# Loading the decay factors first on ScalarE's queue, and making four operand sums one in a slot, in a fused attention and mixture kernel

## The chip, the core and the metric

The kernel runs on one core of one Trainium2 chip. The metric is the device time of one execution in microseconds. Eight runs of the kernel before the change gave a median of 1192.49 us, from 1191.36 to 1193.86.

## The reference

Two computations follow one another, all in 32-bit floats. The first is attention with a decay for each head (4 batches, 8 heads, 768 positions, 64 features), in blocks along the sequence with a running state:

```
intra = (q_b k_b^T * lam^(i-j) for i >= j) v_b
inter = (q_b * lam^(i+1)) kv_state
out_b = intra + inter
kv_state = lam^block * kv_state + (k_b * lam^(block-1-j))^T v_b
```

Its output, rearranged to x of 3072 rows and 512 columns, goes through four experts whose outputs are mixed with normalised probabilities:

```
p = domain_probs / (sum(domain_probs) + 1e-9)
out = sum over e of p[:, e] * (relu(x @ w1[e]) @ w2[e])       # w1: 512x1024, w2: 1024x512
```

## The kernel before

**Units and stages.** Rows come in three groups g of 1024, and a unit (g, e) is one group with one expert. First comes the attention of group 0 (the loop at L1226), then the hidden layer of unit (0,0), written directly (`direct_product`, loop at L1287), then a loop over the twelve units (L1327). While a unit's second product (`second_product`, with w2) runs, the first product (`first_product`, with w1) of the following unit is put between it, and a few steps of the next group's attention as well.

**Seven products for eight.** Every 2x2 block product is made with seven products of sums of blocks, and the first product does that twice, one scheme inside the other. The outer products are M1 to M7; each needs an outer block of x (B11, B21, B22 or a sum T1 to T4, `B_OF`, L86) and from it again four inner sums T3, T1, T2, T4 of quarter blocks of 128x256 (`T_OPS`, L186). For later units these inner sums are made on GpSimd and kept in DRAM. For unit (0,1), the second one, `own_x` (L1095) makes them on VectorE, in place, and returns the views; the products read them straight from SBUF, and a list named `late` stores them to DRAM eight slots afterwards for the units behind (L1125).

**Slots.** A product index i (seven of them in a unit) has eight slots x. In slots 0, 2, 4 and 6 PE makes a part of the second product (eight matmuls), which VectorE adds into `acc` (L909 or L912). In slots 1, 3 and 5 PE makes two inner products of the first product, in slot 7 one. They alternate between two PSUM banks, g1 and g3, and go on accumulating in the same bank: an inner product may begin only when the one two before it has been read out of that bank by VectorE (`m<-pg,m`, L852 by way of L95) or ScalarE (L850). Bank g1 takes the first, third, fifth and seventh.

**What orders VectorE.** Engines work in the order in which the program writes. After the matmuls of a slot and their read-outs, `rest()` takes one step off the list `background` (sums of hidden blocks, attention's masks and scalings), and at the slot's end `pump()` (L143) runs chores that have come due. A chore named `mine[m]` (L1271, L1311 to L1318) makes unit (0,1)'s operands for product m: four sums of w1 on GpSimd and, by `own_x`, four sums of x on VectorE, all written at that one place. `take` (L485) pops the first entry of a list and runs it.

**The beginning.** The loads of q and k for the first two chunks of 128 rows are shared between SyncE's and ScalarE's DMA queues (`load`, L111: the half r = 1 goes through ScalarE for n < 2). After chunk 0's loads ScalarE's queue brings the eight decay factors `lam`, copied to all partitions (L402). VectorE makes from them the mask table `s_decay` (eight scans, L426) and the powers `q_decay` (seven doubling steps, L439). Chunk n goes through `turn` (transposes of q and k, L530), `scores` (L552, then masks `st<-sp,s_decay`) and `values` (L575 to L588); `turn` also writes a scaling `qs<-qT,q_decay` on VectorE and one of k on GpSimd (L505). In the loop `turn` runs one chunk ahead of `scores`, and `scores` one ahead of `values`.

Of the kernel before, what the change touches and what calls it, by code (L numbers as in the profile page):

```python
# [22 lines left out]
def kernel(  # L23
# [30 lines left out]
    nc = tc.nc  # L54
# [88 lines left out]
    def pump(pace=1.0, force=False):  # L143
        while results:
            results.pop(0)()
        while late and (force or late[0][0] <= now[0]):
            late.pop(0)[1]()
        begins = chores and (force or free[0] <= now[0])
        while queue and (force or queue[0][0] <= now[0] or begins and len(queue) > LEFT):
            queue.pop(0)[1]()  # L150
        if begins:
            begin = free[0] = max(free[0], now[0] - 1)
            was = max(busy[0], now[0])
            chores.pop(0)()
            free[0] = max(free[0], begin + max(pace * (busy[0] - was), 1))
# [240 lines left out]
            load(n, "kv")  # L396

    lam_bc = consts.tile([P, H], FP32, name="lam_bc")
    for n, names in ((0, "qk"), (1, "qk"), (0, "v"), (2, "qk"), (1, "v"), (3, "qk")):
        load(n, names)  # L400
        if (n, names) == (0, "qk"):
            nc.scalar.dma_start(out=lam_bc[:], in_=lam.partition_broadcast(P))  # L402
    raw_w1(0, "A11")
    load(2, "v")
    load(3, "v")
# [416 lines left out]
    def first_product(g, e, m, blocks, tags):  # L822

        while (g, e, m) not in fed:
            pump(force=True)
        xs, ws = fed.pop((g, e, m))
        settle(m, blocks)
        old = {
            "M1": None, "M5": None, "M6": blocks.get("M1"), "M2": blocks.get("M1"), "M7": blocks.get("U2"),
            "M3": blocks.get("U4"), "M4": blocks.get("U3"),  # L830
        }[m]
        new = {n: small("m" + n) for n in ("11", "12", "21", "22")} if m in ("M1", "M5", "M6") else old
        banks = {}

        def inner(i):
            t = tags[0] if i in ("M1", "M6", "M5", "M3") else tags[1]
            fresh = i in ("M1", "M7", "M2")
            if fresh:
                banks[t] = bank(t, "p" + t)
            p = banks[t]  # L840
            for j in range(2):
                nc.tensor.matmul(  # L842
                    out=p[:, j * 256:(j + 1) * 256], lhsT=ws[i][:, j * P:(j + 1) * P], rhs=xs[i],
                    start=(fresh and j == 0), stop=True, skip_group_check=True,
                )
            at, begins = READ[i]
            if not begins:
                tt(nc.vector, new[at][:], p[:], new[at][:], ALU.add)
            elif old is None:
                nc.scalar.copy(out=new[at][:], in_=p[:])  # L850
            else:
                tt(nc.vector, new[at][:], p[:], old[at][:], ALU.add)  # L852
            if m in OUT and (at == "12" or not begins):
                nc.scalar.activation(out=new[at][:], in_=new[at][:], func=AF.Relu)  # L854
                if g == LAST:
                    gated(e, *OUT[m], at, new[at])

        return [lambda i=i: inner(i) for i in INNER] + [lambda: finished(g, e, m, blocks, new)]
# [233 lines left out]

    x_tile = {}

    def own_x(m):  # L1095


        name = B_OF[m]
        blk = x_now[name]
        b = {f"B{i + 1}{j + 1}": blk[:, i, j * 256:(j + 1) * 256] for i in range(2) for j in range(2)}  # L1100
        if name in x_tile:
            t = x_tile[name]
            for n, (o, x, y) in {
                "T3": (t[:, 4], "B22", "B12"), "T1": (t[:, 1], "B12", "B11"), "T2": (t[:, 5], "B22", "T1"),
                "T4": (t[:, 6], "B21", "T2"),
            }.items():
                b[n] = o
                tt(nc.vector, o, b[x], b[y], ALU.subtract)
            pieces = ((0, 1), t[:, 0:1]), ((1, 4), t[:, 4:7]), ((4, 7), t[:, 1:4])
        else:  # L1110
            if m == "M1":
                s = [opool.tile([P, 2, 256], FP32, name="acc") for _ in range(2)]
                parts = ((1, 3), s[0][:]), ((3, 5), s[1][:])
                s = [x[:, i] for x in s for i in range(2)]
            else:
                s = stage.tile([P, 4, 256], FP32, name="ops", tag="st")
                parts = (((1, 5), s[:]),)
                s = [s[:, i] for i in range(4)]
            for n, x, y, op in T_OPS:
                b[n] = s[SLOT[n]]  # L1120
                tt(nc.vector, b[n], b[x], b[y], op)
            pieces = (
                ((0, 1), blk[:, 0:1, 0:256]), *parts, ((5, 7), blk[:, 1].rearrange("p (a f) -> p a f", a=2)),
            )
        late.append((now[0] + 8, keep_own(("x", 0, m), x_ops[0, MS.index(m)], pieces)))  # L1125
        return {i: b[B_OF[i]] for i in B_OF}

    def own_w1(m):
# [97 lines left out]
    for i in range(CPG + 2):  # L1226
        if i == 6:
            chores.extend((*prepare_w2(0), *(raw[n] for n in ("A11", "A22", "A21"))))
        more = list(between.get(i, ()))
        order = [(turn, 0), (scores, 1), (values, 2)]  # L1230
        if i == 3:
            order[0:2] = order[1::-1]
        for f, lag in order:
            n = i - lag
            if more and lag == 0 and i < CPG:
                more.pop(0)()
            if 0 <= n < CPG:
                f(n, pairs[n % 3])
            if i < 2 and lag == 0:
                warm(3 - i)  # L1240
            if i == 6 and lag == 2:
                sum_w1(0, "S1", "A21", "A22", ALU.add)
                sum_w1(0, "S3", "A11", "A21", ALU.subtract)
                own_blocks["M1"] = own_x("M1")
            if i == 7 and lag == 2:
                sum_w1(0, "S2", "S1", "A11", ALU.subtract)
                sum_w1(0, "S4", "A12", "S2", ALU.subtract)
            if i == 8 and lag == 0:
                x_sums(("T1", 0))
            if i == 9 and lag == 2:  # L1250
                x_sums(("T1", 1))
            if more and (lag == 2 or i >= CPG):
                more.pop(0)()
            now[0] += 1
            pump()
        while more:
            more.pop(0)()
        if i + 4 < CPG:
            load(i + 4)
        if i < 3:  # L1260
            for name in (("A12",), ("A21",), ("A22",))[i]:
                raw_w1(0, name)
        if i == 5:
            nc.scalar.dma_start(out=probs[:], in_=moe_domain_probs.rearrange("(t p) e -> p t e", p=P))
# [22 lines left out]
    for m in SEQ0[2:]:  # L1287
        if m == SEQ0[-1]:
            for _ in range(2):
                feed2(*fill2.pop(0))  # L1290
        work = direct_product(m, blocks, ("g1", "g3")) if m != "M5" else [m5[1], *m5[3:]]
        for x, f in enumerate(work):
            f()
            for y in sums_then.get((m, x), ()):
                y()
            rest()
            if x < len(work) - 1:
                now[0] += 1
                pump(0.75)
            if m in SEQ0[-2:]:  # L1300
                trickle()
# [25 lines left out]
    for at, (g, e) in enumerate(units):  # L1327
# [14 lines left out]
        for i in range(7):  # L1342
# [30 lines left out]
            for x, part in enumerate(order):  # L1373
                for f in part:
                    if f:
                        f()
                now[0] += 1
                if joins:
                    joined()
                elif (ahead or x % 2 == 0 and x + i) and not (at == len(units) - 2 and i == 6 and x == 7):  # L1380
                    rest()
                if nested or nests:
                    take(aside)
                if nested and ahead and x in (1, 3) and fill3:
                    feed3(*fill3.pop(0))
                if turned_back and x > 0:
                    y = turned_back.pop(0)
                    if y:
                        give(*y[:2], ("s0", "s1"), *y[2:])
                if x == 0 and at * 7 + i >= 6 and fill:  # L1390
                    feed(*fill.pop(0))
                if at == 0 and x == 0 and i < AHEAD:
                    load(CPG + i)
                if steps and (at > 0 or i > 1) and (x == 5 or (x == 2 and i in (1, 3, 5) and at not in (0, 3))):
                    steps.pop(0)()
                if x % 2:
                    trickle()
                pump(PACE[g])
# [32 lines left out]
```

## Time and profile before

| What | Value |
|---|---|
| Median of 8 runs | 1192.49 us (1191.36 to 1193.86) |
| The eight | 1191.36, 1191.47, 1191.71, 1191.95, 1193.04, 1193.13, 1193.23, 1193.86 |
| The profiled execution's own time | 1193.13 us |
| Its span, first to last instruction | 1191.2 us |
| Outside the span | 1.9 us |
| VectorE, GpSimd, ScalarE busy | 67%, 53%, 23% of the span |
| Mean granted TensorE clock | 0.998 of full speed |
| DMA | 324.23 MB, 272 GB/s over the span |

Times in a trace line are the start from the span's begin and the duration, both in microseconds, then engine, line, operation, tile written and tiles read. What stands in square brackets is how long the engine had been idle before and what released it. PE is TensorE, DVE is VectorE, ACT is ScalarE, POOL is GpSimd, SPq and ACTq are the queues that issue DMAs. A clock of 0.50 in a row of windows means that TensorE ran at half speed there.

### The profile page before, as it was taken

To read this page: it belongs to the slowest core of one execution; us is meant where nothing else is said; L and a number is where in the kernel's file an instruction comes from. 1 tells how busy PE (TensorE), PEld (TensorE's weight loads), DVE (VectorE), ACT (ScalarE), POOL (GpSimd) and SP (SyncE) were. 2 spreads that over 40 slices of the span, in tenths; PEclk is the share of its full clock that TensorE was granted. 3 is DMA by queue.
4 is the path that set the end of the run, shared out by engine and by line. 5 is a ranking of instruction groups with operands and counts; after the bars stand their busy time and mean duration, and the time that the engine had idled before them with its cause. 6 is when DMAs were issued, how large, how long until landed. Compare 5 with 4: busy or idle time off the path is not lost.

```text
span 1191.2 us, 17870 instructions
## 1 busy us (share of the span) xinstructions
PE 1179.2 (99%) x6559; PEld 1024.9 (86%) x6559; DVE 793.5 (67%) x1330; ACT 274.7 (23%) x502; POOL 630.8 (53%) x600
## 2 busy tenths in 40 slices
PE   8999999999999999999999999999999999999998
PEld 7888888888888888888888888888888888888887
DVE  6676786468467847647856774773665676777784
ACT  3332122112211201311120120121243342341232
POOL 2666238439457900045344565416584683783884
PEclk9999999999999999999999999999999999999999
DMA  9698799999999997899997989898986657566542
GB/s 226 179 277 241 229 297 319 352 318 351 350 356 325 330 296 226 249 293 298 310 324 244 293 294 308 281 326 281 317 281 248 258 189 271 208 243 239 212 169 79
DMA packets 261927, 324.23 MB, mean 272 GB/s; under 512 B 117296, under 2 KB 203216, under 8 KB 261840
## 3 DMA queue, kind: packets, MB, share of 16 engines
q1 hardware_dynamic: 252288, 320.40, 80.9%
q10 hardware_dynamic: 9552, 2.69, 1.0%
q8 instruction: 52, 0.85, 0.3%
q14 instruction: 35, 0.29, 0.1%
HBM read 237.69 MB, written 89.54 MB: 275 GB/s over the span
## 4 chain that ended last, share of the span: by engine, by line
PE 93%; DVE 3%; DMA 2%; issue 0%; POOL 0%; ACT 0%; ACTq 0%; SPq 0%; DVEq 0%
PE pg L842 38%; PE q L896 31%; PE pq L1068 13%; PE pM L1173 2%; PE sp L552 2%; PE op L580 2%; PE pc L1173 2%; DMA w_ops<-ops 1%; PE op L575 1%; PE op L588 1%; DMA ws_in<-w_ops 1%; DVE m L95 1%; PE pM L1038 1%; PE qp L530 0%; PE kp L530 0%
## 5 line engine op out<-in xcount | busy, mean ns | idle before, releaser
L842 PE MATMUL pg<-xs_in,ws_in 128*128 128x256 f32 x1960 | 469.7, 380 | 0.8 <-DVE m L95 0.8
L842 PEld LDWEIGHTS pg<-xs_in,ws_in 128*128 128x128 f32 x1960 | 371.2, 190 | 52.8 <-DVE m L95 1.8
L95 DVE TENSOR_TENSOR m<-pg,m 128x512 f32<-128x512 f32 x451 | 308.2, 688 | 107.8 <-PE pg L842 100.9
L896 PE MATMUL q<-w2t,hS 128*128 128x256 f32 x1024 | 243.4, 380 | 0.0
L896 PEld LDWEIGHTS q<-w2t,hS 128*128 128x128 f32 x1024 | 193.2, 190 | 27.0 <-issue 0.2
L912 DVE SCALAR_TENSOR_TENSOR acc<-q,gate,acc 128x256 f32<-128x256 f32 x192 | 92.5, 482 | 169.2 <-PE q L896 168.7
L896 PE MATMUL q<-w2t,m 128*128 128x256 f32 x768 | 182.7, 381 | 0.0
L896 PEld LDWEIGHTS q<-w2t,m 128*128 128x128 f32 x768 | 144.8, 190 | 20.5 <-issue 0.3
L854 ACT ACTIVATE m<-m 128x512 f32<-128x512 f32 x132 | 82.9, 630 | 286.2 <-DVE m L95 285.4
L95 POOL TENSOR_TENSOR m<-m,xT 128x512 f32<-128x512 f32 x64 | 80.7, 1277 | 72.7 <-ACT m L854 54.6
L95 POOL TENSOR_TENSOR kn<-kn,s_decay 128x512 f32<-128x512 f32 x20 | 21.9, 1099 | 142.4 <-DMA across<-in_k_dram 78.3
L95 DVE TENSOR_TENSOR sums<-pq,sums 128x256 f32<-128x256 f32 x154 | 64.8, 422 | 45.9 <-PE pq L1068 40.0
L850 ACT COPY m<-pg 128x512 f32<-128x512 f32 x88 | 51.6, 586 | 177.0 <-PE pg L842 174.4
L1068 PE MATMUL pq<-acc,w2t 128*128 128x256 f32 x352 | 86.6, 379 | 0.0
L95 POOL TENSOR_TENSOR ops<-w2b 128x256 f32<-128x256 f32 x24 | 18.1, 776 | 117.8 <-DMA w2b<-in_moe_w_dram 110.8
L1068 PEld LDWEIGHTS pq<-acc,w2t 128*128 128x128 f32 x352 | 66.8, 190 | 9.3 <-issue 0.3
L95 POOL TENSOR_TENSOR acc<-hT,hT 128x512 f32<-128x512 f32 x32 | 40.3, 1274 | 30.9 <-PE pq L1068 29.0
L95 POOL TENSOR_TENSOR w2o<-w2b 128x512 f32<-128x512 f32 x32 | 40.6, 1291 | 22.9 <-DMA w2b<-in_moe_w_dram 16.8
L787 ACT ACTIVATE m<-m 128x512 f32<-128x512 f32 x44 | 27.7, 631 | 101.5 <-DVE m L95 101.5
L95 DVE TENSOR_TENSOR hS<-m,m 128x512 f32<-128x512 f32 x56 | 45.2, 811 | 4.9 <-ACT m L854 4.9
L95 DVE TENSOR_TENSOR m<-m,m 128x512 f32<-128x512 f32 x56 | 47.2, 844 | 0.0
L593 ACT COPY xT<-op 128x256 f32<-128x256 f32 x48 | 17.1, 372 | 120.1 <-PE op L580 114.4
(152 smaller groups left out, 1393.1 us busy)
## 6 DMA issues: line engine op xcount, KB each, us to landing
xs_in<-x_ops SPq DMA_DIRECT2D x70, 896.0 KB, 6.5
ws_in<-w_ops SPq DMA_DIRECT2D x70, 896.0 KB, 8.7
w2t<-w_ops SPq DMA_DIRECT2D x66, 256.0 KB, 6.8
w2t<-w_sums SPq DMA_DIRECT2D x64, 256.0 KB, 3.9
w_ops<-ops SPq DMA_DIRECT2D x28, 512.0 KB, 5.5
w2t<-in_moe_w_dram SPq DMA_DIRECT2D x48, 256.0 KB, 3.7
w2b<-in_moe_w_dram SPq DMA_DIRECT2D x32, 256.0 KB, 5.8
w_sums<-w2o SPq DMA_DIRECT2D x16, 512.0 KB, 4.7
```

Of the source, the lines that this page charges most:

```text
L95: eng.tensor_tensor(out=o, in0=a, in1=b, op=op)
L552: nc.tensor.matmul(out=sp[r][:, ac * C:(ac + 1) * C], lhsT=hc(kT)[half[r], ac], rhs=hc(qT)[half[r], ac], start=True, stop=True,)
L580: nc.tensor.matmul(out=op[r][half[x], a * C:(a + 1) * C], lhsT=vn[:, 4 * r + 2 * a + x], rhs=hc(st[r])[:, 2 * a + x], start=(first and a = ...
L593: nc.scalar.copy(out=xT[:, 2 * r:2 * r + 2, c * C:(c + 1) * C], in_=op[r][:, 0:2 * C].rearrange("p (a t) -> p a t", t=C),)
L787: nc.scalar.activation(out=o[:], in_=o[:], func=AF.Relu)
L842: nc.tensor.matmul(out=p[:, j * 256:(j + 1) * 256], lhsT=ws[i][:, j * P:(j + 1) * P], rhs=xs[i], start=(fresh and j == 0), stop=True, skip ...
L850: nc.scalar.copy(out=new[at][:], in_=p[:])
L854: nc.scalar.activation(out=new[at][:], in_=new[at][:], func=AF.Relu)
L896: nc.tensor.matmul(out=p[:, s * DH:(s + 1) * DH], lhsT=h[A_OF[m]][:, c * 256 + s * P:c * 256 + (s + 1) * P], rhs=fed2[g, e, m][uu][:, c], ...
L912: nc.vector.scalar_tensor_tensor(out=o, in0=x, scalar=w, in1=o, op0=ALU.mult, op1=ALU.add)
L1068: nc.tensor.matmul(out=p[:, 0:256], lhsT=fed3[e, m, x // 2][:, x % 2, c * P:(c + 1) * P], rhs=b[B_OF[i]][:, c * 256:(c + 1) * 256], start= ...
L1173: nc.tensor.matmul(out=p[:, s * 256:(s + 1) * 256], lhsT=a[c][:, f:f + P], rhs=b[:, c, j * 256:(j + 1) * 256], start=(s == 0 and c == 0 an ...
```

## The change

Two edits. The load of `lam` is issued ahead of chunk 0's q and k on ScalarE's queue, where it was third. And `own_x` no longer writes its four sums at once, except for product M1: it puts them on a list `own_sums`, from which the direct stage (L1299) and the first unit (after `rest()`, ahead of the slot's `pump()`) take one in each slot. `first_product` takes all that are still missing of its own product before it uses them, and the store of the operands does so too.

```diff
     lam_bc = consts.tile([P, H], FP32, name="lam_bc")
+    nc.scalar.dma_start(out=lam_bc[:], in_=lam.partition_broadcast(P))
     for n, names in ((0, "qk"), (1, "qk"), (0, "v"), (2, "qk"), (1, "v"), (3, "qk")):
         load(n, names)
-        if (n, names) == (0, "qk"):
-            nc.scalar.dma_start(out=lam_bc[:], in_=lam.partition_broadcast(P))
...
         while (g, e, m) not in fed:
             pump(force=True)
+        while (g, e) == (0, 1) and to_do[m]:
+            take(own_sums, True)
         xs, ws = fed.pop((g, e, m))
...
-    def own_x(m):
+    to_do, own_sums = {}, []
+
+    def own_x(m, at_once=False):
...
+        steps = to_do[m] = []
+
+        def ready():
+            while steps:
+                take(own_sums, True)
+
+        def sub(o, x, y):
+            def f():
+                steps.pop()
+                tt(nc.vector, o, x, y, ALU.subtract)
+
+            steps.append(f)
...
-                tt(nc.vector, o, b[x], b[y], ALU.subtract)
+                sub(o, b[x], b[y])
...
-                tt(nc.vector, b[n], b[x], b[y], op)
+                sub(b[n], b[x], b[y])
...
-        late.append((now[0] + 8, keep_own(("x", 0, m), x_ops[0, MS.index(m)], pieces)))
+        work = list(steps)
+        if at_once:
+            for f in work:
+                f()
+        else:
+            own_sums.extend(work)
+        keep = keep_own(("x", 0, m), x_ops[0, MS.index(m)], pieces)
+        late.append((now[0] + 8, lambda: (ready(), keep())))
         return {i: b[B_OF[i]] for i in B_OF}
...
-                own_blocks["M1"] = own_x("M1")
+                own_blocks["M1"] = own_x("M1", True)
...
                 now[0] += 1
+                take(own_sums)
                 pump(0.75)
...
                     take(aside)
+                if at == 0:
+                    take(own_sums)
```

## The prediction

> **What bounds the kernel now.** I read the page's first row, then the waits of PE, then the chain of waits, the windows and the timeline at the two places where PE waits.
>
> ```profile
> PE 1179.2 (99%) x6559; PEld 1024.9 (86%) x6559; DVE 793.5 (67%) x1330; ACT 274.7 (23%) x502; POOL 630.8 (53%) x600
> ```
>
> ```profile
> PE pg L842 <- DVE m L95: 2.6, 3, 1.8
> PE op L580 <- DVE st L95: 2.4, 3, 2.1
> ```
>
> PE is busy for all but 12 of 1191.2 us, so an edit off PE can only win from those 12 and from a slow clock. Two waits stand out (total, times, longest): 2.1 us for the first mask st, and 1.8 us for one read-out. Everything that shortens them moves the rest forward: no later PE wait is for a DMA.
>
> The first wait, in the chain of waits (start, duration) and in the windows (busy PE, PEld, DVE, ACT, POOL, then the granted clock):
>
> ```profile
> 1.85 3.94 DMA lam_bc<-in_lam_dram
> 5.90 2.63 DVE s_decay L426 x8
> 8.80 0.96 DVE q_decay L439
> 9.78 0.99 DVE q_decay L439
> 11.50 1.05 DVE q_decay L439
> 13.10 0.69 DVE qs L95
> 13.79 1.21 DVE st L95 x2
> ```
>
> ```profile
> 13.00:14.00 1.00, 0.00 (x0) 0.00 (x0) 0.90 (x2) 0.00 (x0) 0.00 (x0) 1.00 0.71 235
> 16.00:17.00 1.00, 1.00 (x19) 0.89 (x16) 0.79 (x2) 0.21 (x1) 0.00 (x0) 0.50 0.39 93
> 17.00:18.00 1.00, 1.00 (x10) 0.99 (x10) 0.42 (x1) 0.37 (x1) 0.00 (x0) 0.50 0.24 56
> ```
>
> DVE works without a break from the landing of lam to the mask, so that landing sets the end. Three of the seven powers take 1 us instead of 0.2 to 0.3, each beside one of POOL's scalings of k. PE ends at 12.34, starts again at 14.45, and a microsecond later its clock is halved; in quarter-microsecond windows it is 0.50 from 15.48 to 18.87. Those 3.39 us cost 1.70 us of PE.
>
> The second wait, in the timeline:
>
> ```profile
> 124.92 0.75 DVE L95 TENSOR_TENSOR ops<-xT 128x256 f32<-128x256 f32 x2
> ...
> 134.71 3.54 DVE L95 TENSOR_TENSOR xt<-xt 128x256 f32<-128x256 f32 x4
> 138.18 0.47 DVE L909 TENSOR_SCALAR acc<-q,gate 128x256 f32<-128x256 f32 x1
> 138.57 0.81 DVE L95 TENSOR_TENSOR m<-m,m 128x512 f32<-128x512 f32 x1
> 139.31 1.28 DVE L95 TENSOR_TENSOR m<-pg,m 128x512 f32<-128x512 f32 x2
> 140.13 1.10 PE L842 MATMUL pg<-ops 128*128 128x256 f32 x4 [1.83 <-DVE m L95]
> ...
> 160.43 3.06 DVE L95 TENSOR_TENSOR xt<-xt 128x256 f32<-128x256 f32 x4
> 163.84 0.48 DVE L912 SCALAR_TENSOR_TENSOR acc<-q,gate,acc 128x256 f32<-128x256 f32 x1 [0.35 <-PE q L896]
> ```
>
> The four sums for M7 come right before a read-out that PE needs. They take 0.87 us each because POOL works then; without POOL a sum costs 0.33 to 0.46 (124.92). The sums for M4 (160.43) hurt nobody: they fill a pause in which PE does attention, and DVE is idle behind them for 0.35 us.
>
> **Part 1: lam first.** Nothing is added; one issue moves ahead of two. ScalarE's issues take 0.51 to 0.55 us, so lam goes out at 0.73 instead of 1.85. It lands at 4.67 if it needs its 3.94 us again, and at 3.2 to 3.7 if it needs the 2.5 to 3.0 us of the first q loads, with no packets ahead of it. I take 4.67, a gain of 1.12. What it moves back: the r = 1 halves of q and k of chunk 0, by 0.53 us. q's would land at about 4.3 against a transpose at 5.37; k's landed at 5.07 and would at 5.6, against 5.80. Chunk 1's issues stay fourth and fifth, and the stall of the fifth (until 3.77) stays. SP's queue isn't touched. So nothing is paid.
>
> DVE then scans from 4.78 to 7.41 and starts the powers at 7.68. POOL's first scaling (1.06 us) starts at 7.55 and blocks the first power until 8.64; its second needs the transposed k of chunk 1, at 8.8, and blocks another until 9.9. The third still comes at 11.33, and by then the other powers (0.18, 0.2, 0.3, 0.43) are done at about 11.1, so one of three collisions goes. qs starts at 11.2 and st at 11.8; PE can start at 12.5 to 12.6. PE's own order allows 12.34. The gain is 1.9 us (1.12 if all three collisions stay, 2.27 if PE never pauses).
>
> **The clock.** The Trainium skill (TensorE: Matmul & The Clock Gate, "Why this matters for your kernels") says that the clock falls after pauses of over about 3 us. By it, a pause of 2.1 us costs no clock, and the change wins nothing there. The row says otherwise: in the 3.4 us before 15.48 PE was idle for 2.3, and the clock fell. The same page's Part 1 says that the activity window runs freely and so differs from run to run; the eight times fit that, four at 1191.4 to 1192.0 and four at 1193.0 to 1193.9, 1.7 us apart, which is half of 3.39. The pause of 1.83 us at 138.3, by my count of such windows from 15.48 inside one, left the clock at 1.00. A pause of at most 1.2 us is below that, so I follow the row: the dip goes in every run. That is 1.70 us against the profiled run and 0.85 against the median.
>
> **What is late next.** PE would come 3.6 us earlier to the transposes of chunk 4, at 20.76 for k instead of 24.36. SP's queue is stuck in one issue for 4.25 us (12.77 to 17.02), so the second half of that k is issued at 18.16 and lands 2.9 us later, at 21.06. PE waits 0.3 us. The raw w1 block lands at 17.1, before its use (22.09 less 3.6). Part 1 and the clock: 1.9 + 1.7 - 0.3 = 3.3 us (2.8 to 3.4).
>
> **Part 2: the sums.** M1 is unchanged. M5's sums are made right before use and are taken together by the force in the first product: no change. M6's go into idle DVE time. The number of sums is the same; only their place changes, so it is a matter of who stands behind each. I went through DVE's and PE's order slot by slot from 118 to 178 us (read-out 0.60 apart, acc 0.40, background 0.60 or 0.80 beside POOL, sum 0.36 or 0.87; 0.20 from PE to DVE, 0.14 back). For the kernel before, this recurrence gives one stall of 2.26 us where the trace has 1.83 and 0.13 shortly after. With the sums spread:
> - M7's stall goes. Its sums fall behind acc and the background step, one to a slot, and the read-outs finish 0.1 to 0.3 us before PE asks.
> - M2's fourth sum now comes at 133.5, beside POOL (0.87), ahead of the read-out that was at 133.51. That ends at 135.04, and PE, due at 134.68, starts at 135.18: 0.50.
> - M4's sums leave the idle pause and go into slots 6 and 7 of their product and 0 and 1 of the next, where DVE is 91% busy (163.7 to 177.7). Two of them beside POOL put the read-out at 168.05, and PE waits 0.69.
> - M3's sums cost 0.07 at most.
>
> So 2.26 goes and 1.26 comes. I scale both by the 1.96 that the trace shows: the gain is 0.8 us. From the other sides: 1.96 if no sum stands in a read-out's way, and -0.2 if each stall doubles. The added force and the store cover the same sums; the store is due eight slots later and they are done in four, so SP's queue waits for nothing new.
>
> **The sum.** 1193.13 - 3.3 - 0.8 = 1189.0 us. Against the median that is 3.5 us or 0.29% (0.2%, or 2.4 us, is about what a measurement of this kernel can tell from no change).
>
> **The rivals.**
> - The spreading costs nothing: 1193.13 - 3.3 - 1.96 = 1187.9. For it: DVE has idle time in most slots. Against: the two dense stretches. 0.15.
> - Only a part comes. All three collisions stay, the pause of 1.0 us still halves the clock in some runs, or the sums' stall only moves: 1192.49 - 1.1 with nothing else is 1191.4, and with half the clock's gain 1190.5. For it: the rule of a free window; DVE is full from 132.3 to 146.8. 0.25, a fifth of it beyond 0.2%.
> - Slower: the sums, beside POOL everywhere and in dense slots, hold up read-outs. A read-out may come 0.7 us late before PE waits (1.73 of the slot between, less 0.2, 0.68 and 0.14), and a sum beside POOL is 0.87. If the sixteen of M2, M7, M3 and M4 cost 13.9 us and 8 of it reach PE, the time is 1187.9 + 8 = 1195.9. It decides from 4.6 us of new stalls on. Against it: POOL idles from 117.8 to 130.6 and from 138.8 to 159.9. 0.05.
> - The change doesn't do what it says: the force in the first product takes all sums in a bunch. Then part 2 gives nothing and the time is 1189.8. But M7 has eight slots for four sums; this lies within the likeliest case's range.
>
> The likeliest case, 1188.4 to 1189.9, has 0.55. Faster by over 0.2% (under 1190.1): 0.55 + 0.15 + 0.05 = 0.75; within 0.2%: 0.20; slower: 0.05. The range goes from 1187.8 to 1190.8 and leaves out some 0.05 below and 0.15 above.
>
> **What would show it.** Right: lam issued at 0.73, the scan starting at 3.3 to 4.8, PE's wait for st under 1.2 us, no clock of 0.50 in the first 40 us, a short wait of kp for k of chunk 4 near 21 us, no wait of 1.8 us near 138 less the shift, and waits of L842 for DVE of 0.3 to 0.7 in the products M2 and M3 of unit (0,1). Wrong: a clock dip that stays with a pause of 1 us; a scan that starts after 5.5 because another thing than the place in the queue delays lam; waits for DVE in unit (0,1)'s products that sum to over 2 us.

## The result and the profile after

The changed kernel takes 1188.76 us (median of 12 runs, 1187.79 to 1189.73). The kernel before, in 32 runs on the same chips, takes 1192.22 us (1190.41 to 1194.17). The ratio is 0.9970, with a 95% interval from 0.9962 to 0.9977: 3.5 us or 0.3% faster, clear of no change. The profiled execution of the changed kernel took 1189.16 us with a span of 1187.3 us. Line numbers after differ from those before by one, and behind `own_x` by more (L842 is L843 here, L530 is L529, L1173 is L1196).

The page's first row and PE's waits after (total, times, longest):

```profile
PE 1178.3 (99%) x6559; PEld 1023.6 (86%) x6559; DVE 791.9 (67%) x1330; ACT 274.7 (23%) x502; POOL 629.0 (53%) x600
```

```profile
PE pg L843 <- DVE m L95: 1.2, 3, 0.5
PE kp L529 <- DMA kn<-in_k_dram: 0.5, 2, 0.4
PE op L579 <- DVE st L95: 0.2, 1, 0.2
```

Both long waits are gone. The first mask is no longer waited for (the 0.2 us for an `st` is a wait between 30 and 100 us that the kernel before has too), and no single wait for a read-out is over 0.5. A wait for k of chunk 4 is new. The beginning, in the timeline after:

```profile
0.73 0.45 ACTq L399 DMA_DIRECT2D lam_bc<-in_lam_dram  x1
4.40 2.63 DVE L425 TENSOR_TENSOR_SCAN s_decay<-lam_bc,ident 128x128 f32<-128x128 f32 x8 [3.40 <-DMA lam_bc<-in_lam_dram]
7.30 3.41 DVE L438 TENSOR_TENSOR q_decay<-q_decay 128x4 f32<-128x4 f32 x7
10.81 0.69 DVE L95 TENSOR_TENSOR qs<-qT,q_decay 128x512 f32<-128x512 f32 x1
11.42 1.28 DVE L95 TENSOR_TENSOR st<-sp,s_decay 128x512 f32<-128x512 f32 x2
12.24 1.39 PE L579 MATMUL op<-st,vn 128*64 128x128 f32 x16
21.05 0.63 PE L529 MATMUL kp<-ident,kn 128*128 128x128 f32 x4 [0.39 <-DMA kn<-in_k_dram]
```

Lam goes out first, the scans start 1.5 us earlier, the seven powers take 3.41 us instead of 4.19 (one meeting with POOL less), and the first values follow the scores at 12.24 without a pause. The windows after (length, busy time of PE, PEld, DVE, ACT and POOL with their instructions, PE's clock, DMA share, GB/s) have no halved clock there:

```profile
13.00:14.00 1.00, 1.00 (x28) 0.96 (x24) 1.00 (x3) 0.37 (x1) 0.00 (x0) 1.00 1.13 318
16.00:17.00 1.00, 1.00 (x22) 0.69 (x22) 1.00 (x2) 0.89 (x2) 0.71 (x1) 1.00 1.09 251
17.00:18.00 1.00, 1.00 (x28) 1.00 (x26) 1.00 (x2) 0.34 (x1) 0.35 (x1) 1.00 0.65 149
```

And unit (0,1)'s sums, in the timeline after:

```profile
123.57 0.41 DVE L95 TENSOR_TENSOR ops<-xT 128x256 f32<-128x256 f32 x1
...
130.23 0.94 DVE L95 TENSOR_TENSOR ops<-xT,ops 128x256 f32<-128x256 f32 x1
131.09 0.68 DVE L95 TENSOR_TENSOR m<-pg,m 128x512 f32<-128x512 f32 x1
131.82 1.13 PE L843 MATMUL pg<-xT,w1b 128*128 128x256 f32 x4 [0.26 <-DVE m L95]
133.43 0.94 DVE L95 TENSOR_TENSOR xt<-xt 128x256 f32<-128x256 f32 x1
134.29 1.28 DVE L95 TENSOR_TENSOR m<-pg,m 128x512 f32<-128x512 f32 x2
136.23 0.41 DVE L95 TENSOR_TENSOR xt<-xt 128x256 f32<-128x256 f32 x1
...
155.61 3.06 DVE L95 TENSOR_TENSOR xt<-xt 128x256 f32<-128x256 f32 x4
```

M7's sums (xt from 133.43) stand singly between read-outs. M2's fourth (130.23) takes 0.94 beside POOL, where the first (123.57) takes 0.41, and holds up the read-out behind it; PE is idle for 0.26 ahead of the inner product that needs it. M4's four at 155.61 are still in one piece.

How far PE is ahead of the kernel before, by the start of the same instructions in the two timelines:

| Instruction | Before | After | Ahead by |
|---|---|---|---|
| kp of chunk 4 | 24.36 (from the chain) | 21.05 | 3.3 |
| first matmul of the second product, unit (0,0) | 93.23 | 89.95 | 3.28 |
| first matmul in unit (0,1)'s product M7 | 149.26 | 144.44 | 4.82 |
| last inner product before the nested group | 883.03 | 878.29 | 4.74 |
| first matmul of the nested group | 883.89 | 879.86 | 4.03 |
| last transpose | 1186.95 | 1182.99 | 3.96 |

So 3.3 us come from the beginning, 1.5 from the sums, and 0.7 is lost at one place near 879 us, where the timeline after says only "issue":

```profile
879.86 1.10 PE L1069 MATMUL pq<-m,w2t 128*128 128x256 f32 x4 [0.50 <-issue]
```

No other profiled run here has that wait, though three of them contain the whole change too. So nothing speaks for the change as its cause; what it was stays open.

### The profile page after: what moved, and what is told of

Read it like the earlier page. It is cut to its first block, busy times and chain, and to the rows that moved or that the text cites. A ratio compares the mean times of both kernels' runs of the same rounds, so it can differ in the third digit from the quotient of the medians.

```text
span 1187.3 us, 17869 instructions
## 1 busy us (share of the span) xinstructions
PE 1178.3 (99%) x6559; PEld 1023.6 (86%) x6559; DVE 791.9 (67%) x1330; ACT 274.7 (23%) x502; POOL 629.0 (53%) x600
## 4 chain that ended last, share of the span: by engine, by line
PE 92%; DVE 3%; SPq 2%; DMA 1%; issue 0%; ACT 0%; ACTq 0%; DVEq 0%
PE pg L843 38%; PE q L897 31%; PE pq L1069 13%; PE pc L1196 2%; PE op L579 2%; PE sp L551 1%; SPq L123 1%; PE pM L1196 1%; DVE hS L95 1%; DVE m L95 1%; PE op L574 1%; DMA w_ops<-w2b 1%; PE op L587 1%; PE pM L1039 1%; SPq L341 0%
## 5 line engine op out<-in xcount | busy, mean ns | idle before, releaser
L843 PE MATMUL pg<-xs_in,ws_in 128*128 128x256 f32 x1960 | 469.7, 380 | 1.0 <-DVE m L95 0.9
L843 PEld LDWEIGHTS pg<-xs_in,ws_in 128*128 128x128 f32 x1960 | 371.2, 190 | 53.0 <-DVE m L95 2.4
L95 DVE TENSOR_TENSOR m<-m,m 128x512 f32<-128x512 f32 x56 | 49.8, 889 | 0.0
L95 POOL TENSOR_TENSOR acc<-hT,acc 128x512 f32<-128x512 f32 x32 | 40.7, 1273 | 7.4 <-PE pq L1069 5.4
```

The costliest lines, as they stand in the source:

```text
L95: eng.tensor_tensor(out=o, in0=a, in1=b, op=op)
L843: nc.tensor.matmul(out=p[:, j * 256:(j + 1) * 256], lhsT=ws[i][:, j * P:(j + 1) * P], rhs=xs[i], start=(fresh and j == 0), stop=True, skip ...
```

## The experiments

The theory: the two edits are separate and add up; the first wins the pause and the clock, the second M7's burst. The rivals: the dip of the clock has another cause; the sums only move the stall. The kernel before was timed beside each set: 1192.23 us for the first four, 1192.38 for the next three, 1193.15 for the last two.

**Lam first, alone.** The diff's first hunk, and nothing else.

> The kernel before with the first edit alone: lam ahead of chunk 0 on ScalarE's queue, the sums still four at once. Theory (the two edits are separate and add up): PE's wait of 2.1 us for the first mask is down to 0.2 at most, no clock of 0.50 after the warm-up, a new wait of kp for the k of chunk 4 of about 0.4 us near 21 us, and the wait of 1.8 us for M7's burst stays. The profile's PE is 3.3 us ahead at chunk 4; the median is some 2.4 us under the kernel before (2.0 to 3.3). Rival (the clock's dip has nothing to do with this pause): the dip stays in about half of the runs and the median is 1.6 us under.

Measured: 1190.24 us, ratio 0.9980 (0.9971 to 0.9989), 2.0 us faster. The pause is gone and M7's wait of 1.8 us is there. At chunk 4 PE waits twice in this profile, and is 2.35 us ahead of before instead of 3.3 (its timeline, PE's rows):

```profile
20.75 0.63 PE L529 MATMUL qp<-ident,qn 128*128 128x128 f32 x4 [0.46 <-DMA qn<-in_q_dram]
22.01 0.63 PE L529 MATMUL kp<-ident,kn 128*128 128x128 f32 x4 [0.63 <-DMA kn<-in_k_dram]
```

The gain is at the lower end of what was expected. In this profile chunk 4's landing took 1.1 us of it back, against 0.4 in the profile of the changed kernel; whether it does so in the other runs is not shown. The interval is 1.3 to 3.5 us, so the median does not tell the theory's 2.4 from the rival's 1.6. What speaks against the rival is the clock, which the third experiment takes up.

**The sums spread, alone.** The changed kernel with the load of lam back in its old place.

> The kernel before with the second edit alone: sums one in a slot, lam where it was. Theory: M7's wait of 1.83 us gives way to one of 0.26 in front of M2's first inner product, so 1.5 us are won at unit (0,1), and the pause of 2.1 us near 13 us stays, with the halved clock in part of the runs. Median 1.5 us under the kernel before. By the recorded prediction's sum for this part it would be 0.8 us, with a wait of 0.7 us in the product M3. Rival (the sums' gain needs the earlier start): below 0.5 us.

Measured: 1190.94 us, ratio 0.9986 (0.9978 to 0.9995), 1.3 us faster. Between 120 and 145 us PE has one wait for a read-out, of 0.3 us. The gains of the two halves, 2.0 and 1.3, add up to 3.3, against 3.5 for both. In this profile lam happened to land earlier than before, and the pause was shorter; the clock still fell, as this kernel's timeline and then its windows show:

```profile
13.75 0.44 PE L580 MATMUL op<-st,vn 128*64 128x128 f32 x4 [1.48 <-DVE st L95]
```

```profile
11.00:14.40 3.40, 1.76 (x24) 1.22 (x22) 3.26 (x6) 0.86 (x2) 1.29 (x1) 1.00 0.99 261
...
14.60:17.70 3.10, 3.10 (x38) 2.98 (x36) 1.92 (x4) 0.74 (x2) 0.00 (x0) 0.50 0.56 127
```

In the 3.40 us from 11.00 PE was busy for 1.76; from 14.60 on its clock is 0.50, until about 17.8.

**The pause filled, the wait left.** PE does dummy matmuls where it was idle:

```diff
+            if i == 2 and lag == 2:
+                warm(7)
             if 0 <= n < CPG:
                 f(n, pairs[n % 3])
```

> The kernel before with seven dummy matmuls of zeros (of 128 columns, as the warm-up's) written on PE ahead of the first values, so that PE is busy in its pause near 13 us while the wait for the mask itself stays; what the kernel computes is the same. Theory (the pause is what halves the clock): no clock of 0.50 from 15.5 to 18.9 in the profile, and none of the upper runs: the median is about 0.85 us under the kernel before, a run with the dip being 1.7 us longer. Rival (the clock falls for another reason, such as the first real load on PE): the dip stays, and the median is that of the kernel before within 0.3 us.

Measured: 1191.53 us (1190.84 to 1192.66), ratio 0.9996 (0.9987 to 1.0004). The median is 0.7 us lower, but the interval holds no change; the scatter is what tells. The fillers are there, the values start at 14.35, nearly as before (14.45), and the clock stays, as this kernel's timeline shows and then its windows of PE alone (length, PE busy, its clock, DMA share, GB/s):

```profile
12.50 1.83 PE L414 MATMUL zp<-xT 128*128 128x128 f32 x14
14.35 0.44 PE L580 MATMUL op<-st,vn 128*64 128x128 f32 x4
```

```profile
11.00:14.40 3.40, 3.38 (x37) 1.00 0.98 242
...
16.00:17.00 1.00, 1.00 (x24) 1.00 0.65 148
```

The runs of the kernel before beside it can be sorted by their mean granted clock. Six of 27 have 0.998 and average 1193.34 us; ten have 1.000 and average 1191.40; a half-speed stretch of 3.4 us in 1191 would lower the mean by 0.0014. (A second such stretch at the kernel's very end, up to 2.3 us of it in these traces, takes up to 0.001 more in any kernel, so 0.998 needs the dip and 0.999 can be either.) With the pause filled no run of eleven has 0.998, the average is 1191.6, and none is over 1192.7 us, where nine of the 27 are over 1193. With lam first none of eleven has 0.998; with the sums alone, where the pause stays, five of eleven. Eleven runs alone could be chance. Taken together, 21 of the 62 runs of the kernel before that the three sets have show 0.998, and none of the 60 runs of the seven kernels in which PE does not pause there. The pause halves the clock, in part of the runs.

**Only M7's sums spread.** All others at once, as before:

```diff
-        if at_once:
+        if at_once or m != "M7":
```

> The changed kernel with only M7's sums one in a slot; those of M5, M6, M2, M3 and M4 are written at once, as before. Theory (only M7's burst cost PE time, and the wait of 0.26 us comes from M2's fourth sum, moved in front of a read-out): no wait of PE for a read-out between 100 and 180 us is left, and the median is 0.2 to 0.3 us under the changed kernel. Rival (spreading the others too is what keeps the read-outs on time): a wait of 0.3 us or more comes at M3's burst, in the second half of the product M2, and the median is the changed kernel's or above.

Measured: 1188.51 us (1187.97 to 1189.55), ratio 0.9965 (0.9952 to 0.9977). In the profile PE has no wait at all between 100 and 200 us. So only M7's burst cost time, and spreading the others is worth nothing. What M2's costs is read better from starts than from idle time, since the matmuls next to a wait run longer too. From the inner product that starts at 120.86 before (117.58 after, 118.18 here) to the first matmul in M7 at 149.26 (144.44, 144.66) PE takes 28.40 us before, 26.86 after and 26.48 here. The other profiles agree with these to 0.01 us, each with those whose sums are placed alike. So spreading M7's sums is worth 1.9 us, and M2's fourth sum takes 0.4 of it back. The difference of 0.25 in the medians is as expected, but smaller than the measurement can tell.

**M4's sums let loose.** M4's sums could not spread, because the first values of group 1 call `until` for every stored product of group 0 (L616 to L618 before), and that forces the chores, M4's operands and their store in one go. The edit lets M4 out of that:

```diff
-                    for m in MS:
+                    for m in [m for m in MS if (g, m) != (1, "M4")]:
                         until(("x", g - 1, m))
```

> The changed kernel, except that the first values of group 1 no longer force the chores up to M4's operands, so that M4's four sums really go one in a slot, into slot 7 of the product M7 and slots 0 to 2 of M3, where VectorE is 91% busy. Theory (the recorded prediction's price for this was right, only the force of the values had been overlooked): PE waits 0.3 to 0.4 us, by the same slot by slot sum, for a read-out in the second half of M3's first two pairs, and the median is 0.3 us above the changed kernel. Rival (the sum was pessimistic, as at M2 where it gave 0.50 and the trace 0.26): no wait of over 0.1 us there and no change of the median.

Measured: 1189.08 us, ratio 0.9977 (0.9967 to 0.9986), 0.3 us above the changed kernel's median in another set of runs, which is not to be told apart. The rival's "no wait of over 0.1 us" is wrong all the same. The timeline of this kernel shows a small part of the wait at M3's second pair, and the larger part one product later than expected, at M4's first inner product:

```profile
161.64 0.94 DVE L95 TENSOR_TENSOR xt<-xt 128x256 f32<-128x256 f32 x1
163.65 0.41 DVE L95 TENSOR_TENSOR xt<-xt 128x256 f32<-128x256 f32 x1
163.98 1.27 DVE L95 TENSOR_TENSOR m<-pg,m 128x512 f32<-128x512 f32 x2
164.80 1.10 PE L843 MATMUL pg<-ops 128*128 128x256 f32 x4
175.02 0.68 DVE L95 TENSOR_TENSOR m<-pg,m 128x512 f32<-128x512 f32 x1
175.75 1.13 PE L843 MATMUL pg<-xt,w1b 128*128 128x256 f32 x4 [0.34 <-DVE m L95]
```

PE is idle for 0.34 us ahead of 175.75. By starts it loses 0.8: from the inner product at 158.65 to the matmuls of the second product at 177.58 it takes 18.93 us, and the changed kernel, from 158.81 to 176.95, takes 18.14. That is more than the 0.3 to 0.4 expected here and near the recorded prediction's 0.69. VectorE, once behind, has no idle time of over 0.15 us left between 160 and 176 us, and most of the price falls due one product later.

**Chunk 4's halves on ScalarE's queue.** This goes at the new wait.

```diff
-                    by = nc.scalar if n < 2 and r == 1 else nc.sync
+                    by = nc.scalar if (n < 2 or n == 4) and r == 1 else nc.sync
```

> The changed kernel with the r = 1 halves of q and k of chunk 4 issued on ScalarE's queue too. Theory (PE's new wait at chunk 4 comes from SyncE's issue that stays stuck for 3 to 4 us): ScalarE issues them by 10 us, SyncE has two issues less, kp of chunk 4 no longer waits, and 0.4 to 1.1 us of PE are won: median 0.4 us or more under the changed kernel, and a narrower spread of its runs. Rival (what holds up the transfers is shared by both queues): ScalarE's issue gets stuck as well, its copies of qT and kT of chunk 1 come late, and PE waits longer than before.

Measured: 1194.89 us, ratio 1.0018 (1.0009 to 1.0026): slower than the kernel before. The rival is right, as the timeline of this kernel shows:

```profile
13.12 0.37 ACTq L123 DMA_DIRECT2D qn<-in_q_dram  x1
14.05 0.38 ACTq L123 DMA_DIRECT2D kn<-in_k_dram  x1
14.46 0.58 ACT L534 COPY qT<-qp 128x512 f32<-128x512 f32 x1 [6.76 <-DMA kn<-in_k_dram]
14.95 0.59 ACT L535 COPY kT<-kp 128x512 f32<-128x512 f32 x1
15.59 1.82 PE L551 MATMUL sp<-qT,kT 64*128 64x128 f32 x16 [4.22 <-ACT kT L535]
```

ScalarE has done its copies of chunk 0 at 7.7, and its next issue waits until 13.12; every copy written behind it waits too. PE loses 4.2 us there, and in the profile its clock is halved from 15.9 to 19.3; the eleven runs' mean clocks are 0.996 to 0.999.

What the issue waits for stands in the trace, in each issue's own record. The loads count their completion on eight counters (semaphores), taken in turn in the order of the program, whichever engine issues. From the ninth load on, an issue waits until the load eight places before it, which used the same counter, has landed. For the issue at 13.12 that is the second half of chunk 3's q, which SyncE issued at 9.71 and which landed at 13.10; for the one at 14.05 it is the second half of chunk 3's k, landed at 14.03. So what both queues share here is the counters: ScalarE stood still for loads of SyncE's queue.

**The same with only M7's sums spread.** Both edits together.

> Both of the versions before that could be better, together: only M7's sums one in a slot, and chunk 4's halves on ScalarE's queue. If both theories hold, neither a wait for chunk 4 nor one for a read-out below 180 us is left: 0.26 + 0.4 us or more, median 1188.1 or less, 0.34% or more under the kernel before. If ScalarE's queue gets stuck, at or above the changed kernel.

Measured: 1193.97 us, ratio 1.0015 (1.0006 to 1.0024), the same failure: PE waits 4.0 us for kT. The wait at M2 is gone, as with M7's sums alone.

**Chunk 4 earlier on SyncE's queue.** The changed kernel, with chunk 4's q and k written ahead of v of chunks 2 and 3:

```diff
     raw_w1(0, "A11")
+    load(4, "qk")
     load(2, "v")
...
-            load(i + 4)
+            load(i + 4, "qkv" if i else "v")
```

> The changed kernel with chunk 4's q and k issued on SyncE's queue ahead of v of chunks 2 and 3 (they were behind), right after w1's first block; the number of loads is the same. Theory (PE's wait at chunk 4 is only the place of that load in a saturated queue): q and k of chunk 4 land before 20 us, PE waits for none of them, and the stuck issue falls on v of chunk 2 or 3, which PE needs only at 22 us or later; 0.4 to 1.1 us are won and the runs lie closer together: median 0.4 us or more under the changed kernel. Rival (the stuck issue only moves on): v of chunk 2 lands after 23 us and PE waits for it as long as it did for chunk 4.

Measured: 1188.37 us (1186.82 to 1188.88), ratio 0.9961 (0.9948 to 0.9975). In the profile PE waits for nothing from 8 to 36 us. SyncE's issues there, in this kernel's timeline (a row is a group of issues):

```profile
12.34 0.98 SPq L123 DMA_DIRECT2D qn<-in_q_dram  x2
13.37 2.02 SPq L123 DMA_DIRECT2D kn<-in_k_dram  x2
15.43 3.06 SPq L118 DMA_DIRECT2D vn<-in_v_dram  x3
```

Chunk 4 is in time, as the theory has it. The long issue of 2.9 us (4.3 before) has not moved to a v, though: the rows are of two and three issues, and the longest of them takes 1.5 us. That this order is faster than the changed kernel is not shown: the intervals against the kernel before overlap, and the runs lie no closer together. The profiled run is the fastest of the five, 2.3 us ahead of the changed kernel's, but at k of chunk 4 it is only 0.6 ahead (20.47 against 21.05); the rest comes from waits later on, where the two kernels are alike.

**The same with only M7's sums spread.**

> The same order of loads together with only M7's sums one in a slot. If both edits hold, PE waits neither for chunk 4 nor for a read-out below 180 us: 0.26 + 0.4 us or more, median 1188.1 or less, about 0.35% under the kernel before. If the stuck issue only moves on, the median of the version with only M7's sums, 1188.5.

Measured: 1188.08 us (1186.99 to 1189.36), ratio 0.9961 (0.9948 to 0.9973). The lowest median of all, but in this profile k of chunk 3 was late by 0.51 us at 16.53, and the interval overlaps with those of all three versions that it builds on.

## Why the prediction was right

**Lam's landing.** The prediction took the later of two estimates, 4.67; the scans start at 4.40 instead of 4.78. The reckoning with POOL, that one of three meetings goes, is right (3.41 us for the powers instead of 4.19). With both, PE has no pause ahead of the first values, the end of the range that was given as 2.27 and not taken; their start moved by 2.21 us, from 14.45 to 12.24, instead of 1.9.

**What is moved back.** "So nothing is paid" holds for the end, but not as worked out. "SP's queue isn't touched" and "the stall of the fifth (until 3.77) stays" are wrong, because of the shared counters. SyncE's fifth issue, v of chunk 0, waits for SyncE's first load; it comes at 4.48 instead of 3.28, and by chunk 4's q the queue is 1.1 us later (13.87 instead of 12.77). ScalarE's fifth now waits for lam and comes at 4.32. In all profiles SyncE's fifth comes at 3.3 to 3.5 with lam third and at 4.4 to 4.6 with lam first; why the first load lands later behind lam is open. The first transposes came at 5.60 instead of 5.37, and k of chunk 0 was waited for (0.15 us). All this is hidden because the scores of chunk 0 start at 9.04, as before (9.06).

**The clock.** As far as the mean clocks tell, the dip is gone in every run whose kernel has no pause, as predicted. One argument for it was weak: that a pause of 1.83 us had left the clock alone was taken to mean that 1.2 us is safe. With the sums alone, a pause of 1.48 us and one of 0.16 behind it, in 3.4 us, were enough to halve it. That this step came out right is luck, since the pause went altogether. Against the Trainium skill (TensorE: Matmul & The Clock Gate, "Why this matters for your kernels"), with its pauses of over about 3 us, the rows decide: pauses of 1.5 and 2.1 us did it.

**Chunk 4.** The wait was foreseen, at its place and with 0.3 us; the profile has 0.39 of idle time, which by starts is 0.55 (k follows q by 0.44 before and by 0.99 after). PE came 3.86 us earlier to q of chunk 4 (20.06 instead of 23.92), not 3.6, and the two misses cancel to the 3.3 that was forecast. With lam alone the waits were 1.1, so the figure is one draw of a landing that varies.

**The sums.** The mechanism and the sign were right, and the size was half: 0.8 was forecast (0.87 by its own figures), 1.5 measured (4.82 less 3.28). M7's burst cost 1.9 us, as the scaled sum had it (1.96). Of the new stalls, M2's 0.50, scaled to 0.43, measured 0.4; M3's 0.07 is nowhere to be seen. The step that failed is M4's, "leave the idle pause and go into slots 6 and 7 of their product and 0 and 1 of the next", with its 0.69 us: these sums did not move, because the first values of group 1 force them. Without the terms of M4 and M3 the prediction's sum gives 1.5. The price itself was of the right size: when the sums were let loose by one more edit, PE lost 0.8.

**The sum.** 1189.0 was forecast for the median and for the profiled run's reckoning alike. The beginning gave 3.3 as forecast, the sums 0.7 more, and the wait near 879 us took 0.7 back in the profiled run: 1189.16. That this run fits so well is luck. The median, 1188.76, is 3.5 us under the median before, as forecast.

What is not settled: what makes runs with no dip differ by up to 2 us (the changed kernel's 1187.79 to 1189.73). Their mean clocks do not tell them apart. The profiles show two places, though each profile is one run. Up to chunk 4 the landing of the early loads makes 0.4 to 1.1 us, and in three profiles the first transposes still run slowly (1.1 us for four instead of 0.6), and the scores of chunk 0 start at 9.3 to 9.4 instead of 9.0. From there to 200 us the profiles agree to some 0.05 us where their code does. Between 200 and 883 us, where the code is the same in all, they take from 682.2 to 683.6 us, mostly by single waits of PE for a read-out such as the one of 0.4 us near 398 us in the changed kernel. What sets off those waits is open.

## What to carry to other kernels

On an engine that is busy for 99% of the span, list its few waits and ask of each which single item ends it; a load of 4 KB, third in its queue, cost 2.1 us of PE and in part of the runs 1.7 more by the clock. Work spread out one to a slot helps only where a burst stood in front of a read-out that was due; before pricing a move, look for every call that forces the list, since M4's sums never moved. And a DMA issue on a compute engine's queue holds up everything written behind it for as long as it waits itself; here it waited for loads of the other queue, and two loads of 128 KB cost 4.2 us of PE. Before moving a load, count which earlier load its issue will wait for.

## What the hardware showed that was not expected

The clock fell after 3.4 us in which PE was busy for 1.76, with a longest pause of 1.48 us, but not after the pause of 1.83 us near 138 us in the kernel before. In the clock's record the half-speed stretch lasts 3.41 us in each of the four profiles with a dip, and the full-speed stretch ahead of it 10.24, three times as long. Counted on in steps of 3.413 us from the dip, the pause near 138 us falls into a stretch (138.36 to 141.77) in which PE is busy for 1.64 us, less than the 1.76 that halved the clock. So neither the length of a pause nor PE's busy time decides alone. The matmuls differ (full 128x128 ones against attention's, many of them with 64 rows or columns), but no run here tests that.

The issues of the two DMA queues are tied together by the eight counters that they take in turn: with lam moved to the front of ScalarE's queue, SyncE's queue ran 1.1 us late by chunk 4. SyncE's issue of 2.7 to 4.5 us near 13 us (in nine profiles) is another thing: the load that it waits for had landed 0.8 us or more before it began, and what held it is open.
